# Symmetric scores computed once and transposed by DMA, attention accumulated transposed, feed-forward placed after each batch

## The chip, the core and the metric

The kernel runs on one core of a Trainium2 chip. The metric is the device time of one execution in microseconds (us). PE is the tensor engine (matmuls), PEld its weight loads, ACT the scalar engine, DVE the vector engine, POOL the general engine, SP the sync engine, which here does nothing but issue DMAs from its queue. The granted clock is the share of its full clock that PE was given in a stretch of time, 1.00 at most. A DMA is issued on its queue and lands some microseconds later. "L174" is line 174 of the kernel that the view belongs to, so the numbers differ from kernel to kernel.

## The reference

Per batch (8 batches, 3008 rows, width 256, `z` of width 64), an attention without softmax is gated by `u`; the 24064 rows that result go through a feed-forward layer of width 2048.

```python
scores = (1.0 / S) * np.matmul(z, z.transpose(0, 2, 1))
attn = np.maximum(scores, 0.0) ** 2
out = u * np.matmul(attn, v)
x = out.reshape(B * S, D)
h = x @ w_in
g = h * (1.0 / (1.0 + np.exp(-1.702 * h)))
return (g @ w_out).astype(np.float32)
```

The scores are `z` times its own transpose, so they are symmetric, and so is their squared positive part. Half of them would do.

## The kernel before

It runs in two stages: attention for all batches, with the gated result written to DRAM; then the feed-forward over blocks of 512 rows, each read back by two DMA transposes. A "unit" is 128x1024 scores: four key chunks of 128 for 256 queries. A unit is made by four matmuls with 64 contraction rows, in two pairs, each pair using the upper and the lower half of the array at once. ACT or DVE evicts it with a ReLU, and DVE or POOL squares it.

```python
        def scores(t):                       # 576 units
            # ... cut
            for p in range(2):
                for r_ in range(2):
                    j = 4 * q + 2 * p + r_
                    h0 = r_ * DQK
                    pe.matmul(sc[:, r_, p, :], ZT[h0:h0 + DQK, j * P:(j + 1) * P],
                        ZT[h0:h0 + DQK, isup * ISUP:(isup + 1) * ISUP], start=(p == 0), stop=(p == 1))
            if (t + 1) % DVE_RELU_EVERY == 0:
                dve.tensor_scalar(r, sc, 0.0, csc, ALU.max, ALU.mult)
            else:
                act.activation(r, sc, AF.Relu, scale=csc)
            (pool if (t + 1) % POOL_SQ_EVERY == 0 else dve).tensor_tensor(ap_, r, r, ALU.mult)   # abridged

        def attend(t):                       # the squared scores are the weights, V streams
            # ... cut
            for ib in range(NIBS):
                pe.matmul(O[:, ib, :], ap_[:, r_, p, ib * P:(ib + 1) * P], V16[:, j, :],
                    start=(j == 0 and ib == 0), stop=(j == NJ - 1 and ib == NIBS - 1))
            # ... after the last key chunk: X = O * u on DVE, and X goes to DRAM
```

Of the kernel before, what the change touches and what calls it, by code (L numbers as in the profile page):

```python
# [11 lines left out]
P = 128  # L12

DVE_RELU_EVERY = 5
POOL_SQ_EVERY = 4


@with_exitstack
def kernel(
# [8 lines left out]
):  # L28
    nc = tc.nc
# [10 lines left out]
    SPAD = NJ * P  # L40
    ISUP = 512
    NIS = SPAD // ISUP
    NIBS = ISUP // P
    NJP = NJ // 2
    NTOK = B * S
    TB = 512
    NTB = (NTOK + TB - 1) // TB
    NCC = D // P
    NFF = DFF // P
    NK = D // P  # L50
    NFG = 8
    FFG = NFF // NFG
    assert NTOK % P == 0

# [3 lines left out]
    dve = nc.vector  # L58
    act = nc.scalar
    pe = nc.tensor  # L60
    sp = nc.sync
    pool = nc.gpsimd

    const = ctx.enter_context(tc.tile_pool(name="const", bufs=1))
    ident = const.tile([P, P], F16, name="ident")
    make_identity(nc, ident)
    W1 = const.tile([P, NK, DFF], F16, name="W1")
    W2 = const.tile([P, NFF, D], F16, name="W2")

    dramp = ctx.enter_context(tc.tile_pool(name="dramp", bufs=1, space=bass.MemoryType.DRAM))  # L70
    xdram = dramp.tile([NTOK, D], F16, name="xdram")

    pxt = ctx.enter_context(tc.tile_pool(name="pxt", bufs=4))
    XTs = [None] * (NTB + 1)
    TBCs = [0] * (NTB + 1)

    def load_xt(tb, eng):
        if tb >= NTB or XTs[tb] is not None:
            return
        TBC = min(TB, NTOK - tb * TB)  # L80
        TBCs[tb] = TBC
        XT = pxt.tile([P, NCC, TB], F16, name="XT", tag="XT")
        XTs[tb] = XT
        for cc in range(NCC):
            eng.dma_start_transpose(  # L85
                XT[:, cc, :TBC],
                xdram[tb * TB:tb * TB + TBC, cc * P:(cc + 1) * P],
            )

    ISUP = 256  # L90
    NIS = SPAD // ISUP
    NIBS = ISUP // P
    UNITS = NJ // 4
    NU = NIS * UNITS
    GRP = 3
    LAG = 2 * GRP
    ZG = 8

    with (
        tc.tile_pool(name="pa", bufs=2) as pa,  # L100
        tc.tile_pool(name="pa1", bufs=1) as pa1,
        tc.tile_pool(name="pr", bufs=7) as pr,
        tc.tile_pool(name="ps_sc", bufs=3, space=bass.MemoryType.PSUM) as ps_sc,
        tc.tile_pool(name="ps_o", bufs=2, space=bass.MemoryType.PSUM) as ps_o,
        tc.manual_schedule(engines={mybir.EngineType.PE}),
    ):
        loads = {}
        zts = {}
        Xd = {}

        def load_batch(b):
            if b >= B:
                return
            zst = pa1.tile([P, NJ, DQK], F32, name="zst", tag="zst")
            vst = pa1.tile([P, NJ, D], F32, name="vst", tag="vst")
            if SREM:
                pool.memset(zst[SREM:, NJ - 1, :], 0.0)  # L117
                pool.memset(vst[SREM:, NJ - 1, :], 0.0)  # L118
            half = NJ // 2
            zd = z[b, :S0].rearrange("(n p) d -> p n d", p=P)  # L120
            sp.dma_start(zst[:, :half, :], zd[:, :half, :])
            sp.dma_start(zst[:, half:NJ - 1, :], zd[:, half:, :])
            if SREM:
                sp.dma_start(zst[:SREM, NJ - 1, :], z[b, S0:S].unsqueeze(1))
            sp.dma_start(vst[:, :NJ - 1, :], v[b, :S0].rearrange("(n p) c -> p n c", p=P))
            if SREM:
                sp.dma_start(vst[:SREM, NJ - 1, :], v[b, S0:S].unsqueeze(1))
            zst16 = pa.tile([P, NJ, 2, DQK], F16, name="zst16", tag="zst16")
            for h in range(2):
                js = slice(h * half, (h + 1) * half)  # L130
                for c in range(2):
                    dve.tensor_copy(zst16[:, js, c, :], zst[:, js, :])  # L132
            V16 = pa.tile([P, NJ, D], F16, name="V16", tag="V16", bufs=3)
            X = pa.tile([P, NJ, D], F16, name="X", tag="X")
            zts[b] = pa.tile([P, SPAD], F16, name="ZT", tag="ZT")
            casts = [(V16[:, 4 * q:4 * (q + 1), :], vst[:, 4 * q:4 * (q + 1), :]) for q in range(NJ // 4)]
            loads[b] = (zst16, V16, casts)
            Xd[b] = X

        def zt_part(b, g):  # L140
            zst16 = loads[b][0]
            ztp = ps_o.tile([P, ZG, P], F16, name="ztp", tag="O")
            for jj in range(ZG):
                pe.transpose(ztp[:, jj, :], zst16[:, g * ZG + jj, :, :], ident)  # L144
            act.activation(zts[b][:, g * ZG * P:(g + 1) * ZG * P], ztp, AF.Copy, scale=1.0)  # L145

        def v_cast(b):
            casts = loads[b][2]
            if casts:
                o, i_ = casts.pop(0)  # L150
                dve.tensor_copy(o, i_)  # L151

        def load_u(b, isup):
            ru = pa.tile([P, NIBS, D], F32, name="ru", tag="ru", bufs=4)
            lo = isup * ISUP
            hi = min(S, lo + ISUP)
            nfull = (hi - lo) // P
            sp.dma_start(
                ru[:, :nfull, :],
                u[b, lo:lo + nfull * P].rearrange("(n p) c -> p n c", p=P),  # L160
            )
            rem = (hi - lo) - nfull * P
            if rem > 0:
                sp.dma_start(ru[:rem, nfull, :], u[b, lo + nfull * P:hi].unsqueeze(1))
                pool.memset(ru[rem:, nfull, :], 0.0)
            return ru

        aps = {}
        Os = {}
        us = {}  # L170

        def scores(t):
            b, k = divmod(t, NU)
            isup, q = divmod(k, UNITS)  # L174
            ZT = zts[b]
            if q == 0:
                us[(b, isup)] = load_u(b, isup)
            sc = ps_sc.tile([P, 2, 2, ISUP], F32, name="sc", tag="sc")
            for p in range(2):
                for r_ in range(2):  # L180
                    j = 4 * q + 2 * p + r_
                    h0 = r_ * DQK
                    pe.matmul(  # L183
                        sc[:, r_, p, :],
                        ZT[h0:h0 + DQK, j * P:(j + 1) * P],
                        ZT[h0:h0 + DQK, isup * ISUP:(isup + 1) * ISUP],
                        start=(p == 0), stop=(p == 1),
                    )
            r = pr.tile([P, 2, 2, ISUP], F16, name="r", tag="r")
            if (t + 1) % DVE_RELU_EVERY == 0:  # L190
                dve.tensor_scalar(r, sc, 0.0, csc, ALU.max, ALU.mult)  # L191
            else:
                act.activation(r, sc, AF.Relu, scale=csc)  # L193
            ap_ = pr.tile([P, 2, 2, ISUP], F16, name="ap_", tag="ap_", bufs=11)
            aps[t] = ap_
            if (t + 1) % POOL_SQ_EVERY == 0:
                pool.tensor_tensor(ap_, r, r, ALU.mult)
            else:
                dve.tensor_tensor(ap_, r, r, ALU.mult)

        def attend(t):
            b, k = divmod(t, NU)
            isup, q = divmod(k, UNITS)
            ap_ = aps.pop(t)
            V16 = loads[b][1]
            if q == 0:
                Os[isup] = ps_o.tile([P, NIBS, D], F32, name="O", tag="O")
            O = Os[isup]
            for p in range(2):
                for r_ in range(2):  # L210
                    j = 4 * q + 2 * p + r_
                    for ib in range(NIBS):
                        pe.matmul(  # L213
                            O[:, ib, :],
                            ap_[:, r_, p, ib * P:(ib + 1) * P],
                            V16[:, j, :],
                            start=(j == 0 and ib == 0), stop=(j == NJ - 1 and ib == NIBS - 1),
                        )
            if q == UNITS - 1:
                X = Xd[b]  # L220
                ru = us.pop((b, isup))
                dve.tensor_tensor(X[:, isup * NIBS:(isup + 1) * NIBS, :], O, ru, ALU.mult)  # L222
                del Os[isup]
                if isup == NIS - 1:
                    sp.dma_start(
                        xdram[b * S:b * S + S0].rearrange("(n p) c -> p n c", p=P),
                        X[:, :NJ - 1, :],
                    )
                    if SREM:
                        sp.dma_start(xdram[b * S + S0:(b + 1) * S].unsqueeze(1), X[:SREM, NJ - 1, :])  # L230

        load_batch(0)
        for g in range(NJ // ZG):
            zt_part(0, g)
        load_batch(1)
# [114 lines left out]
```

## Time and profile before

| | before |
|---|---|
| time, median (range) | 1458.07 us (1457.97 to 1458.94), 3 runs |
| attention, as counted here (scores begin at 13.4 us, the first matmul with V comes at 21.9) | 26 to 766 us |
| feed-forward, as counted here (its first groups run from 765.8 us) | 776 to 1452 us |
| PE busy, whole span | 95% |

The first view is the page of the kernel before: the busy row of PE (us, share of the span, instructions), and the chain of work that ended last, by engine.

```profile
PE 1380.4 (95%) x11616; PEld 996.3 (68%) x11616; DVE 1177.3 (81%) x1195; ACT 847.4 (58%) x863; POOL 305.1 (21%) x176
...
PE 79%; DVE 11%; DMA 4%; issue 3%; ACT 2%; ACTq 1%; SPq 0%; DVEq 0%
```

Next the windows view of the kernel before, for its two stages: window, its length, busy us of each engine, granted clock, DMA share, GB/s.

```profile
26.00:766.00 740.00, 692.94 (x7029) 548.82 (x7030) 659.47 (x709) 454.99 (x474) 301.05 (x165) 0.97 0.31 88
776.00:1452.00 676.00, 673.62 (x4500) 439.22 (x4499) 507.18 (x470) 378.63 (x376) 0.00 (x0) 1.00 0.18 53
```

PE is the limit in both stages. In attention DVE is nearly as full: 659 of 740 us. A busy PE is not yet a PE at its best rate, so the rate has to be read from starts. The timeline of PE of the kernel before gives them (start, busy, what; in brackets the idle time before, and who ended it):

```profile
499.99 0.83 PE L183 MATMUL sc<-ZT 64*128 64x256 f16 x12
500.75 1.05 PE L213 MATMUL O<-V_3991,ap__6715 128*128 128x256 f16 x8
...
513.96 0.99 PE L183 MATMUL sc<-ZT 64*128 64x256 f16 x12 [3.44 <-DVE r L191]
```

Six score pairs take 500.75 - 499.99 = 0.76 us. The last line shows PE waiting 3.44 us for an eviction on DVE: that is what a full DVE costs.

### The profile page before, as it was taken

Reading aid. Unit: us, or ns where it says so; the run is one execution under the profiler, and the core shown is the slowest. Engines: PE = TensorE matmul, PEld = TensorE weight load, DVE = VectorE, ACT = ScalarE, POOL = GpSimd, SP = SyncE. Lnnn points to the kernel's source line nnn. Section 1 sums busy time; section 2 is a strip of 40 time slices with the busy share of each in tenths; the row PEclk is TensorE's granted clock in tenths of the full one; section 3 lists DMA queues with packets and bytes.
Section 4 is the critical chain, followed back from the end, with each engine's and each line's share of the span. In section 5 each row is a group of like instructions: output and inputs, shape, how many; then the busy total and the mean of one; then the engine's idle time right before and its main releaser. Section 6 shows DMA issues by size and latency. Waiting matters only on the chain.

```text
span 1456.5 us, 27175 instructions
## 1 busy us (share of the span) xinstructions
PE 1380.4 (95%) x11616; PEld 996.3 (68%) x11616; DVE 1177.3 (81%) x1195; ACT 847.4 (58%) x863; POOL 305.1 (21%) x176
## 2 busy tenths in 40 slices
PE   5888899999999999999997999999999999999998
PEld 3566677777777777777784666666666666666666
DVE  5989789898999988988985877777777777787775
ACT  4455565665666656666655556555555656565553
POOL 2333344343444433434340000000000000000000
PEclk9899899999999999999999999999999999999999
DMA  9734425124251111212102121211111111112111
GB/s 295 214 117 126 118 50 164 38 67 146 57 164 37 57 51 36 80 37 69 46 21 62 54 66 48 62 51 59 51 59 52 58 52 59 54 56 64 48 49 44
DMA packets 175691, 110.69 MB, mean 76 GB/s; under 512 B 78545, under 2 KB 174801, under 8 KB 175313
## 3 DMA queue, kind: packets, MB, share of 16 engines
q1 hardware_dynamic: 123632, 92.42, 21.2%
q10 hardware_dynamic: 51136, 12.33, 3.8%
q0 software_dynamic: 800, 4.19, 0.8%
q8 instruction: 91, 1.49, 0.4%
q14 instruction: 32, 0.25, 0.1%
HBM read 59.64 MB, written 36.96 MB: 66 GB/s over the span
## 4 chain that ended last, share of the span: by engine, by line
PE 79%; DVE 11%; DMA 4%; issue 3%; ACT 2%; ACTq 1%; SPq 0%; DVEq 0%
PE O L213 26%; PE hg L284 24%; PE yps L309 22%; PE sc L183 7%; DVE r L191 2%; DMA vst<-in_v_dram 2%; ACT r L193 1%; DVE X L222 1%; DMA xdram<-X 1%; ACTq L85 1%; DMA zst<-in_z_dram 1%; DVE V_1333 L151 0%; DVE zst_7973 L132 0%; DVE V_6649 L151 0%; DVE V_3991 L151 0%
## 5 line engine op out<-in xcount | busy, mean ns | idle before, releaser
L193 ACT ACTIVATE r<-sc 128x1024 f16<-128x1024 f32 x461 | 443.1, 1024 | 256.1 <-PE sc L183 237.0
L291 ACT ACTIVATE tsg<-hg 128x1024 f16<-128x1024 f32 x376 | 379.6, 1023 | 286.0 <-PE hg L284 180.9
L292 DVE TENSOR_TENSOR GT<-hg,tsg 128x1024 f16<-128x1024 f32 x376 | 447.0, 1221 | 113.6 <-ACT tsg L291 111.1
L284 PE MATMUL hg<-XT,W_63 128*128 128x512 f16 x1504 | 371.5, 379 | 9.6 <-DVE GT L292 9.5
L309 PE MATMUL yps<-W_64,GT 128*128 128x256 f16 x3008 | 374.1, 273 | 0.0
L309 PEld LDWEIGHTS <-GT 128*128 128x128 f16 x3008 | 294.2, 98 | 94.0
L284 PEld LDWEIGHTS <-W_63 128*128 128x128 f16 x1504 | 146.3, 97 | 151.3 <-issue 27.6
L183 PE MATMUL sc<-ZT 64*128 64x256 f16 x2304 | 165.0, 275 | 32.5 <-DVE r L191 24.2
L183 PEld LDWEIGHTS <-ZT 64*128 64x128 f16 x2304 | 98.5, 95 | 83.1 <-issue 71.5
L191 DVE TENSOR_SCALAR r<-sc 128x1024 f16<-128x1024 f32 x115 | 139.4, 1213 | 8.5 <-PE sc L183 8.5
L315 DVE TENSOR_SCALAR ysb<-yps 128x512 f32<-128x512 f32 x94 | 64.5, 686 | 64.5 <-PE yps L309 64.5
L222 DVE TENSOR_TENSOR X<-O,ru 128x512 f16<-128x512 f32 x96 | 65.3, 680 | 6.8 <-PE O L213 6.8
L145 ACT ACTIVATE ZT<-ztp 128x1024 f16<-128x1024 f16 x24 | 24.4, 1023 | 36.2 <-PE ztp L144 36.2
L144 PE MATMUL ztp<-ident,zst_97 128*128 128x128 f16 x24 | 2.9, 312 | 10.5 <-DVE zst_97 L132 10.5
L132 DVE CAST zst_97<-zst 128x768 f16<-128x768 f32 x4 | 2.1, 557 | 9.9 <-DMA zst<-in_z_dram 9.9
L144 PEld LDWEIGHTS <-zst_97 128*128 128x128 f16 x24 | 2.4, 144 | 10.8 <-DVE zst_97 L132 10.8
L291 ACT ACT_TABLE_LOAD x1 | 1.3, 1283 | 14.2 <-DMA xdram<-X 14.2
L118 POOL MEMSET vst<- 64x256 f32 x8 | 2.8, 344 | 27.5 <-DVE V_1333 L151 6.0
L117 POOL MEMSET zst<- 64x64 f32 x8 | 1.2, 146 | 30.5 <-DVE zst_97 L132 9.5
L151 DVE CAST V_1333<-vst 128x1024 f16<-128x1024 f32 x6 | 5.6, 966 | 0.9 <-DMA vst<-in_v_dram 0.9
L151 DVE CAST V_102<-vst 128x1024 f16<-128x1024 f32 x6 | 3.8, 689 | 2.9 <-DMA vst<-in_v_dram 2.9
L151 DVE CAST V_5320<-vst 128x1024 f16<-128x1024 f32 x6 | 5.6, 962 | 0.0
(1766 smaller groups left out, 1875.5 us busy)
## 6 DMA issues: line engine op xcount, KB each, us to landing
out_dram<-ysb SPq DMA_DIRECT2D x47, 512.0 KB, 2.9
vst<-in_v_dram SPq DMA_DIRECT2D x8, 2944.0 KB, 12.2
ru<-in_u_dram SPq DMA_DIRECT2D x88, 256.0 KB, 2.7
xdram<-X SPq DMA_DIRECT2D x8, 1472.0 KB, 7.0
zst<-in_z_dram SPq DMA_DIRECT2D x8, 384.0 KB, 4.0
zst<-in_z_dram SPq DMA_DIRECT2D x8, 352.0 KB, 4.8
w1s<-in_moe_w_in_dram POOLq DMA_DIRECT2D x1, 2048.0 KB, 10.6
w2s<-in_moe_w_out_dram POOLq DMA_DIRECT2D x1, 2048.0 KB, 12.0
```

The source lines that it names most:

```text
L145: act.activation(zts[b][:, g * ZG * P:(g + 1) * ZG * P], ztp, AF.Copy, scale=1.0)
L151: dve.tensor_copy(o, i_)
L183: pe.matmul(sc[:, r_, p, :], ZT[h0:h0 + DQK, j * P:(j + 1) * P], ZT[h0:h0 + DQK, isup * ISUP:(isup + 1) * ISUP], start=(p == 0), stop=(p = ...
L191: dve.tensor_scalar(r, sc, 0.0, csc, ALU.max, ALU.mult)
L193: act.activation(r, sc, AF.Relu, scale=csc)
L213: pe.matmul(O[:, ib, :], ap_[:, r_, p, ib * P:(ib + 1) * P], V16[:, j, :], start=(j == 0 and ib == 0), stop=(j == NJ - 1 and ib == NIBS - 1),)
L222: dve.tensor_tensor(X[:, isup * NIBS:(isup + 1) * NIBS, :], O, ru, ALU.mult)
L284: pe.matmul(hg[:, e, :TBC], W1[:, k, ff * P:(ff + 1) * P], XT[:, k, :TBC], start=(k == 0), stop=(k == NK - 1),)
L291: act.activation(tsg[:, :, :TBC], hg[:, :, :TBC], AF.Sigmoid, scale=1.702 / FSC)
L292: dve.tensor_tensor(GT[:, fg * FFG:(fg + 1) * FFG, :TBC], hg[:, :, :TBC], tsg[:, :, :TBC], ALU.mult,)
L309: pe.matmul(yps[:, s2, :], GT[:, ff, s * P:(s + 1) * P], W2[:, ff, :], start=(ff == 0), stop=(ff == NFF - 1),)
L315: dve.tensor_scalar(ysb[:, yy * 2:yy * 2 + ns2, :], yps[:, :ns2, :], 1.0 / FSC, None, ALU.mult)
```

## The change

The intent: compute a score unit only where the key chunk is not before the query chunk (336 units of 128 keys x 2 by 512 queries instead of 576), and get the mirrored ones by a DMA transpose from SBUF to SBUF. Let the squared scores stream (512 columns) and V be the weights, so that the output is accumulated transposed, which is the layout that the feed-forward wants; the trip through DRAM goes. Run the feed-forward after each batch, its first nine groups inside the last query chunk, and the next batch's first score units under its end. V's casts go to POOL, output evictions to ACT. The core of the diff, cuts marked:

```diff
+    def load_z(b):
+        # ... z by POOL's queue with a cast, written twice side by side
+        sp.dma_start_transpose(ZT[b], zst.rearrange("p n c d -> p (n c d)"))
+    def load_u(b, i):
+        # ... four DMAs of 64-column runs on SP, then 32x32 transposes on DVE
-            if (t + 1) % DVE_RELU_EVERY == 0:
+            if dve_relu and n == 2:
                 dve.tensor_scalar(rl, sc, 0.0, csc, ALU.max, ALU.mult)
             else:
                 act.activation(rl, sc, AF.Relu, scale=csc)
+            a = pa.tile([P, 2, CH], F16, name="a", tag="a", bufs=21)
+            (pool if sq[0] % 4 == 0 else dve).tensor_tensor(a, rl, rl, ALU.mult)
+            cj = jp // 2
+            if cj > i:
+                # ... t: the transposed tile of (i, cj)
+                if cj < NCH - 1:
+                    sp.dma_start_transpose(
+                        t[:, k0:k0 + 2].rearrange("p r g c -> p (r g) c"),
+                        a.rearrange("p r c -> p (r c)"),
+                    )
+                else:
+                    for r in range(2):
+                        sp.dma_start_transpose(t[:, :, k0 + r, :], a[:, r, :])
+    def weights(b, i, j):
+        cj, g = divmod(j, CB)
+        if cj >= i:
+            return unit[b, i, j // 2][:, j % 2, :width(i)]
+        t = TT[b, cj, i]
+        # ... the 512 columns of the mirrored unit
-                            O[:, ib, :],
-                            ap_[:, r_, p, ib * P:(ib + 1) * P],
-                            V16[:, j, :],
+                acc[c][:, :n], V16[b][:, j, c, :], weights(b, i, j),
+    SCHED = {
+        0: [(4, 3), (14, 3), (23, 2), (34, 2)],
+        # ... at which attention step of chunk i how many units of chunk i + 1 are computed
+    }
+    for b in range(B):
+        for i in range(NCH):
+            # ... attention of chunk i; in the last chunk, an up group at every fifth step
+        # ... load_z, load_v, load_u of the next batch
+        for q in range(HEAD, nup):
+            up_group(b, q)
+            if q >= LAGY:
+                down(b, *downs.pop(0))
+        while downs or nxt:
+            if nxt and n % 3 == 0:
+                scores(b + 1, nxt.pop(0), True)
+            if downs:
+                down(b, *downs.pop(0))
+            n += 1
-        xdram = dramp.tile([NTOK, D], F16, name="xdram")   # and its stores and transposes
```

A unit whose mirror lies in an ordinary query chunk is transposed whole (eight blocks of 128x128); one whose mirror lies in the last, short chunk in two halves (four blocks each). Per batch that is 20 whole and 20 half transposes, all issued by SP.

## The prediction

> **What bounds it now.** The tensor engine. The page's busy table has PE at 95% (DVE 81%, ACT 58%), and the chain that ended last is 79% PE. By stages (windows table, chain in order of time): 26 us of start, attention to 766 us, 10 us of hand-over (X to DRAM 6.5 us), feed-forward to 1452 us at 99% PE busy. In the timeline of PE, 24 attention matmuls of 256 columns take 2.73 us (114 ns each) and 6 score pairs 0.76 us (127 ns a pair). Attention therefore owes PE 4608 x 114 = 524 us plus 1152 x 127 = 146 us, 670 of its 740 us. The rest is a clock of 0.91 early on and waits for DVE, which in attention is 89% busy: evictions of 1.21 us, and squares of 0.68 us that grow to about 2.4 us beside Pool's.
>
> **What changes.**
> - Score units (128x1024) fall from 576 to 336. Score pairs now have 512 columns: 336 x about 235 ns (estimate from 127 ns at 256) = 79 us, saving 67.
> - Attention becomes 47 matmul slots of 512 columns per query chunk: 48 x 47 x 216 ns, less the short last chunks, = 477 us, saving 47. 216 ns is the trace's feed-forward rate at 512; the Trainium skill, "TensorE: Matmul & The Clock Gate", section "Back-to-back issue gap", has the same (N/2.4+2.5).
> - 240 evictions (1.02-1.21 us) and 240 squares go away; V casts go to Pool, output evictions to ACT.
> - The X round trip through DRAM and the hand-over go: 8 us. Feed-forward PE work is unchanged, about 680 us.
> - Added: 160 whole and 160 half-unit DMA transposes, all issued by SP. The trace's XT transposes, half a unit each, occupy their issuing queue 1.25 us; ordinary issues 0.38 us. If the excess scales with bytes, a whole unit takes 2.1 us: 20 x 2.1 + 20 x 1.25 = 67 us of SP per batch, about 90 with the other loads, in an attention phase of 75-80 us that starts with some of it done. Bandwidth suffices: XT moved 12.3 MB in 3.8% of 16 engines' span, 223 GB/s (the skill's "DMA: Bandwidth & Descriptors", section "Latency and other measured facts", has 261 GB/s); 63 MB need about 280 us of the span. Query chunks 3 and 4 should wait for the freshest, 0-10 us per batch.
> - Start: z through Pool's queue, one large transpose, twelve units of scores, V casts on Pool: about 38 us before attention streams, 12 worse.
>
> **Sum.** 477 + 79 + 680 = 1236; plus start 38, batch changes 8 x 3 = 24, transposes 8 x 3 = 24: about 1322 us.
>
> **Predicted: 1320 us, 8 in 10 between 1262 and 1390. Faster by over 2%: 0.89; within 2%: 0.05; slower: 0.06.**
>
> **What would show each step.** Right: PE at least 91% busy; attention matmuls 216 ns apart, 47 us less; PE score work about 80 us; DVE below 70% in attention; gaps of several us before attention matmuls, once or twice per batch, released by a DMA into the transposed tiles, with SP's queue nearly solid then; whole transposes near 2.1 us on the queue. Wrong: PE waiting for ACT or DVE inside attention, or a gap at each batch boundary.
>
> **What would make it wrong.** SBUF-to-SBUF transposes costing 3 us or more on SP: the queue would then be the limit, attention about 110 us per batch, and the gain mostly gone. Cheaper transposes with a smooth start give 1270. Pool's V casts holding DVE's squares, or a fuller PE being granted a lower clock, would cost tens of us.

## More of the kernel before

A program on one core gives one time per run; all runs told of here agree within about 1% with the others of their kernel and are counted as fast.

The feed-forward leaves the order of its matmuls to the scheduler:

```python
        for tb in range(NTB + 1):
            # ... load_xt(tb + 1): two DMA transposes of 512x128 from DRAM
            for fg in range(NFG):            # "up": 4 matmuls of 512 columns, a sigmoid, a product
                # ... cut
                act.activation(tsg, hg, AF.Sigmoid, scale=1.702 / FSC)
                dve.tensor_tensor(GT[:, fg * FFG:(fg + 1) * FFG, :TBC], hg, tsg, ALU.mult)
            # ... "down" of block tb - 1: 64 matmuls of 256 columns, evicted by DVE
```

Last, a piece of the chain of the kernel before in its feed-forward (start, length, what):

```profile
903.51 0.22 PE yps L309 x2
903.73 0.91 PE hg L284 x4
904.64 0.22 PE yps L309 x2
...
904.86 1.02 PE hg L284 x4
...
908.26 5.35 PE yps L309 x49
```

The scheduler's order runs up groups in bursts, with only two or three down matmuls between them, and then 49 down matmuls in a row. Within a burst a group of four comes every 1.1 to 1.4 us, about as fast as DVE can take its products (1.22 us each on the page).

## The result, and the profile after

| | before | after |
|---|---|---|
| time, median (range) | 1458.02 us (1457.44 to 1458.94), 4 runs | 1305.53 us (1304.05 to 1308.17), 4 runs |
| ratio of fast runs | | 0.8956 (95%: 0.8939 to 0.8972) |
| PE busy | 1380.4 us | 1249.3 us |

A ratio is the mean time of one kernel's fast runs over that of the other's of the same rounds, so it is not quite the ratio of the medians quoted. Of the 152 us between the medians, 131 are busy time of PE. The kernel before was timed again; its median lay between 1455.2 and 1457.9 us.

The page of the kernel after: the same two rows.

```profile
PE 1249.3 (96%) x7520; PEld 680.3 (52%) x7520; DVE 844.5 (65%) x820; ACT 728.8 (56%) x786; POOL 266.9 (20%) x237
...
PE 92%; DVE 2%; DMA 1%; POOL 1%; issue 1%; ACT 1%; ACTq 1%; SPq 0%; POOLq 0%
```

The windows of one batch of the kernel after, its attention and its feed-forward; columns as above.

```profile
517.20:595.00 77.80, 76.94 (x386) 32.10 (x385) 46.52 (x52) 39.09 (x41) 23.18 (x15) 1.00 0.88 151
595.00:675.20 80.20, 79.24 (x567) 53.42 (x565) 60.02 (x52) 52.47 (x59) 10.65 (x14) 1.00 0.33 92
```

A batch takes 158.0 us, and all of it is PE: 76.9 of 77.8 us and 79.2 of 80.2 us. DVE is at 46.5 of 77.8 us in attention, 60%, so it no longer paces PE. The lower clock that the prediction named as a danger did not come: 0.992 over the run, against 0.985 before. The chain of the kernel after gives the rates:

```profile
1176.84 0.75 PE sc L126 x6
...
1192.58 0.54 PE sc L126 x4
1193.12 0.21 PE o L186 x2
1193.34 10.03 PE o L174 x46
...
1226.07 0.86 PE hg L222 x4
1226.93 0.87 PE yp L245 x8
```

An attention matmul of 512 columns takes 10.03 / 46 = 218 ns. Three score pairs take 0.75 us, two take 0.54. The feed-forward is now an even 0.865 + 0.87 = 1.735 us per up group and half down tile, eight of which serve 512 rows: 13.88 us, against (1452 - 776) / 47 = 14.4 us before.

The sum of tensor work by these rates: attention 48 x 47 x 0.218, less 10 for the short last chunks, 482 us; scores 8 x (10 x 0.75 + 6 x 0.54) = 86 us (ten groups of three pairs and six of two in each batch); feed-forward 47 x 13.88 = 652 us. Together 1220 us. The first attention matmul is at 32.5 us, and the first batch is 10.8 us longer than a later one (168.8 against 158.0). At the seven batch ends PE waits 18 us in all for evictions and products (1.9 us at four of them, 3.3 to 3.6 at three). That makes 1281 us. The remaining 24 us or so are small losses that I did not break down.

Three views of the kernel after concern the transposes. The first is the whole list of PE's waits (total us, times, longest):

```profile
PE sc L126 <- DMA ZT<-zst: 19.6, 1, 19.6
PE sc L126 <- ACT rl L136: 19.5, 18, 4.3
PE o L174 <- POOL V_96 L97: 5.3, 3, 2.6
PE sc L126 <- DVE gt L231: 4.8, 7, 1.0
PE sc L126 <- DVE rl L134: 3.2, 9, 0.6
```

No wait of an attention matmul (`o`) for a transposed tile (`tt`) is among them. The second is the queue of SP in time, in the same batch (start, time from the first issue to the end of the last, DMAs):

```profile
511.70 13.11 SPq L148 DMA_TRANSPOSE tt<-a  x8
524.91 5.14 SPq L154 DMA_TRANSPOSE tt<-a  x4
530.16 8.66 SPq L148 DMA_TRANSPOSE tt<-a  x6
538.93 5.13 SPq L154 DMA_TRANSPOSE tt<-a  x4
...
569.26 5.14 SPq L154 DMA_TRANSPOSE tt<-a  x4
574.45 1.64 SPq L111 DMA_DIRECT2D uq<-in_u_dram  x3
576.40 3.78 SPq L81 DMA_TRANSPOSE ZT<-zst  x1
580.28 4.68 SPq L111 DMA_DIRECT2D uq<-in_u_dram  x7
```

A row joins issues of one line and includes the short waits between them. Taken one by one, issues fill 66.7 of the 73.3 us from 511.7 to 585, nearly the whole attention of the batch, and the longest pause is 1.1 us. The queue ends in time. The third gives the duration of one issue on that queue in ns (minimum/median/maximum), for the whole units, the halves and z:

```profile
L148 SPq DMA_TRANSPOSE tt<-a x160: 1231/1279/5829, 25.1 to 1191.3; - x160
...
L154 SPq DMA_TRANSPOSE tt<-a x160: 1188/1257/2715, 53.0 to 1204.2; - x160
...
L81 SPq DMA_TRANSPOSE ZT<-zst x8: 3684/3873/5561, 11.8 to 1048.9; - x8
```

Eight blocks cost 1.28 us and four blocks 1.26 us: halving a transpose of this size saves nothing. Twenty-four blocks cost 3.87 us, 0.16 us a block. The prediction had scaled with bytes from four blocks to eight and got 2.1 us.

### The profile page after: what moved, and what is told of

It is laid out like the page before. It is cut to its first block, busy times and chain, and to the rows that moved or that the text cites. A ratio compares the mean times of both kernels' runs of the same rounds, so it can differ in the third digit from the quotient of the medians.

```text
span 1306.3 us, 19043 instructions
## 1 busy us (share of the span) xinstructions
PE 1249.3 (96%) x7520; PEld 680.3 (52%) x7520; DVE 844.5 (65%) x820; ACT 728.8 (56%) x786; POOL 266.9 (20%) x237
## 3 DMA queue, kind: packets, MB, share of 16 engines
q1 hardware_dynamic: 405760, 119.07, 45.4%
## 4 chain that ended last, share of the span: by engine, by line
PE 92%; DVE 2%; DMA 1%; POOL 1%; issue 1%; ACT 1%; ACTq 1%; SPq 0%; POOLq 0%
PE o L174 36%; PE hg L222 25%; PE yp L245 25%; PE sc L126 6%; PE o L186 1%; DVE rl L134 1%; DVE gt L231 1%; POOL a L140 1%; DMA W_58<-in_moe_w_in_dram 1%; ACTq L260 1%; DMA zst<-in_z_dram 1%; ACT sg L230 0%; POOL V_96 L97 0%; DVE a L140 0%; DMA vst<-in_v_dram 0%
## 5 line engine op out<-in xcount | busy, mean ns | idle before, releaser
L231 DVE TENSOR_TENSOR gt<-hg,sg 128x1024 f16<-128x1024 f32 (+1 forms) x384 | 460.4, 1200 | 182.4 <-ACT sg L230 181.0
L230 ACT ACTIVATE sg<-hg 128x1024 f16<-128x1024 f32 (+1 forms) x384 | 386.0, 1005 | 274.6 <-PE hg L222 271.5
L136 ACT ACTIVATE rl<-sc 128x1024 f16<-128x1024 f32 x304 | 291.4, 1024 | 282.7 <-PE sc L126 256.0
L245 PE MATMUL yp<-W_59,gt 128*128 128x256 f16 x3008 | 383.0, 273 | 0.0
L222 PE MATMUL hg<-xt,W_58 128*128 128x512 f16 (+1 forms) x1408 | 354.5, 374 | 0.0
L245 PEld LDWEIGHTS <-gt 128*128 128x128 f16 x3008 | 292.5, 98 | 104.3 <-issue 7.5
L140 POOL TENSOR_TENSOR a<-rl 128x1024 f16<-128x1024 f16 x84 | 166.2, 1979 | 717.1 <-ACT rl L136 700.2
L140 DVE TENSOR_TENSOR a<-rl 128x1024 f16<-128x1024 f16 x252 | 230.9, 939 | 98.1 <-ACT rl L136 95.1
L222 PEld LDWEIGHTS <-W_58 128*128 128x128 f16 x1536 | 150.3, 98 | 108.7
L126 PE MATMUL sc<-ZT 64*128 64x512 f16 x672 | 104.7, 394 | 47.1 <-DMA ZT<-zst 19.6
L114 DVE STREAM_TRANSPOSE ut<-uq 128x1024 f32<-128x1024 f32 (+1 forms) x48 | 58.6, 1220 | 54.1 <-DMA uq<-in_u_dram 53.2
L174 PEld LDWEIGHTS <-V_96 128*128 128x128 f16 x276 | 26.3, 100 | 43.9 <-issue 10.1
L174 PEld LDWEIGHTS <-V_2475 128*128 128x128 f16 x276 | 26.3, 99 | 35.4 <-issue 7.6
L174 PEld LDWEIGHTS <-V_8743 128*128 128x128 f16 x276 | 26.1, 99 | 35.1 <-issue 7.1
L174 PEld LDWEIGHTS <-V_5609 128*128 128x128 f16 x276 | 25.9, 98 | 34.3 <-issue 5.3
L174 PEld LDWEIGHTS <-V_10321 128*128 128x128 f16 x276 | 25.9, 98 | 33.9 <-issue 5.3
L174 PEld LDWEIGHTS <-V_919 128*128 128x128 f16 x276 | 25.9, 98 | 33.9 <-issue 5.3
L174 PEld LDWEIGHTS <-V_7187 128*128 128x128 f16 x276 | 25.9, 98 | 33.9 <-issue 5.3
```

What stands on the lines that cost most here:

```text
L114: dve.transpose(ut[:, :, :n // QW, :].rearrange("p k q t -> p q k t"), uq[:, :n // QW])
L126: pe.matmul(sc[:, r, :], zt[h, 2 * jp + r, :], zt[h, i * CB:(i + 1) * CB, :], start=True, stop=True,)
L136: act.activation(rl, sc, AF.Relu, scale=csc)
L140: (pool if sq[0] % 4 == 0 else dve).tensor_tensor(a, rl, rl, ALU.mult)
L174: pe.matmul(acc[c][:, :n], V16[b][:, j, c, :], weights(b, i, j), start=(c == 0 and j == 0), stop=(c == 1 and j == NJ - 2),)
L222: pe.matmul(hg[:, e, :n], W1[:, c, ff * P:(ff + 1) * P], XT[b, i][:, c, :n], start=(c == 0), stop=(c == NCC - 1),)
```

## The experiments

Twelve kernels ran, all built on the kernel after except two. Theory A: the gain is tensor-engine work removed, together with waits. Rivals: B, it is the relief of ACT and DVE; C, it is the overlap of the stages. A further question was how close the SP queue is to being the limit.

### All scores computed, nothing transposed

```diff
-            if cj > i:
+            if False:
-        if cj >= i:
+        if True:
             return unit[b, i, j // 2][:, j % 2, :width(i)]
-        return [(i, jp) for jp in range(2 * i, NU)]
+        return [(i, jp) for jp in range(NU)]
+    SCHED = {i: [(4, 2), (12, 2), (19, 2), (26, 2), (33, 2), (40, 2)] for i in range(NCH - 1)}
-            if dve_relu and n == 2:
+            if (n == 2) if dve_relu else (jp % 4 == 3):
                 dve.tensor_scalar(rl, sc, 0.0, csc, ALU.max, ALU.mult)
     # and a: 26 buffers for 21, tt/gt: 11 for 14
```

> The changed kernel with all 576 score units computed and no unit transposed; the transposed accumulation and the order of the stages stay. Theory A (the gain is tensor-engine work): 240 more score pairs at 0.25 us each give +60 us, so 1350 to 1390 us, PE still over 93% busy. Theory B (the gain is mostly relief of ScalarE and VectorE, which then pace attention again): over 1420 us, with PE waiting for evictions inside attention. Attention per batch was 78 us; A says about 86, B over 92.

Measured: 1398.64 us (1397.95 to 1399.70), +93 us, between the two. A quarter of the units made during attention are evicted by DVE here, so that ACT does not carry all the added ones. The page's busy row of this kernel:

```profile
PE 1336.9 (96%) x8000; PEld 678.1 (49%) x8000; DVE 1172.4 (84%) x1120; ACT 854.7 (61%) x906; POOL 423.6 (30%) x297
```

PE's waits for evictions, from the waits view of the same kernel (total us, times, longest):

```profile
PE sc L126 <- ACT rl L136: 13.1, 20, 3.2
PE sc L126 <- DVE rl L134: 8.0, 24, 0.4
```

PE is busy 88 us longer (1336.9 against 1249.3) and still at 96%, and all its waits for ACT and DVE come to 28.3 us, against 27.5 in the kernel after. So these 93 us are tensor work: A holds for them, and B does not explain them. But the 84% of DVE is an average over stages. Inside attention DVE is full in this run: in the window from 560 to 618.5 us it is busy 58.36 of 58.50 us, PE 57.18. PE waits for it only about 0.36 us per query chunk there; with much less tensor work DVE would probably have paced the stage. The relief of DVE is thus not what the 93 us are made of, but without it they would probably not have come out whole. The 93 us exceed the 60 us expected of A because the pairs now come in groups of two, at 0.54 us a group: each batch has 30 groups of two where it had six of three and six of two inside attention, 16.2 - 7.7 = 8.5 us, 68 us in eight batches. The 18 groups more per batch also delay the matmuls behind them: seven attention matmuls after a group take 1.62 us from start to start, about 0.1 us more than seven in a long run, which makes some 15 us (an estimate from these two rates). About 10 us are not broken down. So the reuse of symmetry is worth 93 us, and the rest of the change about 59 us (1457.39 to 1398.64).

### Each whole transpose issued as two halves

```diff
-                    sp.dma_start_transpose(
-                        t[:, k0:k0 + 2].rearrange("p r g c -> p (r g) c"),
-                        a.rearrange("p r c -> p (r c)"),
-                    )
+                    for r in range(2):
+                        sp.dma_start_transpose(t[:, k0 + r], a[:, r, :])
```

> Each whole-unit transpose issued as two half-unit ones: same bytes, 60 issues of about 1.26 us per batch on the SP queue in place of 40, so a whole unit costs about 2.5 us of the queue, a little more than the prediction's 2.1 us. If the measured 1.28 us is why no wait for transposes was seen, but the prediction's model of the waits holds, the chunks 3 and 4 now wait up to 13 us per batch: +40 to +110 us. If the queue has slack that the model missed: within 1% of the changed kernel (1295 to 1320 us).

Measured: 1461.87 us (1460.14 to 1465.01), +156 us, above the 40 to 110 us expected. The whole gain is gone, with the same arithmetic and the same bytes. The queue of SP in the timeline of this kernel:

```profile
596.01 16.35 SPq L149 DMA_TRANSPOSE tt<-a  x12
612.47 5.13 SPq L152 DMA_TRANSPOSE tt<-a  x4
617.69 1.06 SPq L111 DMA_DIRECT2D uq<-in_u_dram  x2
618.86 10.36 SPq L149 DMA_TRANSPOSE tt<-a  x8
```

PE in the timeline of the same kernel:

```profile
625.32 1.87 PE L172 MATMUL o<-tt,V 128*128 128x512 f16 x4 [9.38 <-DMA tt<-a]
640.20 5.30 PE L172 MATMUL o<-tt,V 128*128 128x512 f16 x16 [3.27 <-DVE xt L194]
```

And its windows view around the first of these waits:

```profile
610.00:650.00 40.00, 27.35 (x114) 10.71 (x112) 7.05 (x9) 6.67 (x7) 3.49 (x3) 0.83 0.54 111
```

The queue is solid, and PE waits 9.4 us for a transposed tile, at the fourth query chunk, which is where the prediction had looked for it. The second wait is named a gate on DVE; the u that the gate needs comes over the same queue, behind the transposes (that link is read from the order of the queue, not tested). The DMA engines are at 54% in this window, and over the run the packets of SP's queue took no more of their time than before (39.6% of 1463 us, against 45.4% of 1306), so it is issue time and not bandwidth that is short. There is a second cost: in the gaps the granted clock falls (0.83 in this window; 0.953 over the run against 0.992), and the same 7520 matmuls are busy 1286.1 us in place of 1249.3, 37 us more. The Trainium skill, "TensorE: Matmul & The Clock Gate", Part 1, describes this: an idle PE drops to half its clock, and comes back only after some microseconds of work. The trace agrees: the granted clock is 0.50 from 620.0 to 630.2 us, that is from within the 9.4 us wait until about 5 us after it, and the first four matmuls after the wait take 1.87 us, where four take 1.03 elsewhere. The 156 us add up from PE's waits and this: 40 us for transposed tiles and 43 for gates (neither occurs in the kernel after), 22 more for ACT's evictions, 14 for products, and the 37 us of slower matmuls.

### Each whole transpose issued twice

```diff
+                    dup = pa.tile([P, 8, P], F16, name="dup", tag="dup", bufs=3)
+                    sp.dma_start_transpose(dup, a.rearrange("p r c -> p (r c)"))
                     sp.dma_start_transpose(
```

> Each whole-unit transpose issued a second time into a scratch tile: the same 60 issues per batch as with the split, and 42 MB more moved. If issue time on the queue is what could matter, it costs what the split costs, within 10 us. If bandwidth of the 16 DMA engines matters (they are 60% busy per batch now), it costs at least 30 us more than the split, and landing takes longer than the present 3.3 us.

Measured: 1533.38 us (1532.87 to 1536.67), +228 us, and 72 us more than the split. The expectation of "within 10 us" failed: with as many issues, more bytes cost more. In the batch looked at the DMA share was 0.85 to 0.91 for 80 us of attention, and the median issue of the second copy 1.33 us. The median landing of the halves did not change (2.5 us), that of the whole ones went from 3.3 to 3.4 us. Bytes count once the engines are this full, though I can't separate the queue's slower issues from the scratch tiles' reuse (three buffers).

### The same bytes through another queue

```diff
+                    dup = pa.tile([P, 8, P + 8], F16, name="dup", tag="dup", bufs=2)
+                    pool.dma_start(dup[:, :, :P], a.rearrange("p r (g c) -> p (r g) c", c=P))
```

> The changed kernel with every whole unit copied once more, as 1024 runs of 256 bytes, by an ordinary DMA issued by Pool: the bytes of the run with each whole transpose issued twice, with the SP queue's issues left as they were. If the queue's issue time alone makes attention wait: within 15 us of 1305. If the DMA engines' time counts as well (that run cost 72 us more than the split at the same number of issues, and with all feed-forward last the DMA share was 100% in attention): +30 to +100 us, with transposes taking longer than 1.28 us of the queue.

Measured: 1464.61 us (1461.09 to 1473.83), +159 us, but inconclusive. The median whole transpose on SP's queue grew from 1.28 to 1.93 us, so bytes do slow the queue. However, POOL issued the copies in its own order, between its squares, and PE waited 87 us for POOL's squares. The run does not say how much of the 159 us belongs to the bytes.

### No overlap of the stages at the ends of a batch

```diff
-    HEAD = 9
+    HEAD = 0
-            if nxt and n % 3 == 0:
+            if nxt and not downs:
```

> The changed kernel without the overlap of stages: no feed-forward group inside the last query chunk, and the first twelve score units of the next batch only after the last down-projection. Theory A: only the twelve units' evictions become exposed, about 8 us at each of 7 batch ends: +40 to +75 us. Theory C (overlap of attention with feed-forward is the main source of the gain): over +100 us, with gaps spread over the feed-forward stage too. If the overlap is worth nothing: within 15 us of 1305.

Measured: 1366.62 us (1365.82 to 1369.14), +61 us, within A's range. From the waits view of this kernel:

```profile
PE sc L126 <- ACT rl L136: 42.5, 56, 4.3
```

The kernel after has 19.5 us and 18 times on this line; the waits that came are at the batch ends. The granted clock is 0.971, and PE is busy 29.5 us longer with the same matmuls (1278.8 us). Overlap at the ends is worth 61 us, but it is not the main source.

### All feed-forward after all attention

```diff
+    XD = dramp.tile([B * NCH, P, NCC, CH], F16, name="XD")
     # ZT and V16: two buffers; tt/gt 13 for 14; xt 5 for 8; the next batch's z and V loaded in its chunk 2
-        5: [],
+        5: [(4, 3), (14, 3), (23, 3), (34, 3)],      # the next batch's first units
+            act.dma_start(XD[b * NCH + i][:, :, :n], XT[b, i][:, :, :n])
     # ... all feed-forward in one loop at the end, its blocks read back from XD
```

> The changed kernel with its parts kept, but all attention first and all feed-forward after it, as in the kernel before: the gated output goes through DRAM already transposed, and the next batch's first twelve score units lie inside the last query chunk. If the place of the feed-forward is worth nothing in itself: 1285 to 1315 us, as batch ends lose their 4 us gaps. If the feed-forward's real service is the time it leaves to the SP queue (about 71 us of issues per batch, against 70 us of tensor work per batch in attention alone): attention waits for transposes as in the split, 1330 to 1400 us, with the queue nearly solid and PE gaps released by a transpose or by the late u loads behind them.

Measured: 1434.90 us (1432.75 to 1436.83), +129 us, above the 1330 to 1400 us expected: nearly all of the gain goes. Attention alone now takes about 91 us per batch ((760 - 35) / 8). The windows view of this kernel within attention:

```profile
300.00:600.00 300.00, 241.07 (x1158) 93.33 (x1158) 130.02 (x160) 123.54 (x130) 99.74 (x90) 0.91 1.03 185
```

PE's two longest waits in that attention, from the waits view:

```profile
PE o L176 <- DVE xt L198: 58.3, 18, 7.6
PE o L176 <- DMA tt<-a: 49.1, 7, 8.7
```

The DMA share is 103% (the packets' times, summed and divided by the time of 16 engines: by this measure nothing is left), PE is busy 80% of the time at a clock of 0.91. In the kernel after the share averages 60% over a batch, 88% in attention and 33% in the feed-forward. So the feed-forward of each batch is the time in which loads and transposes catch up. That placing it there is worth over 100 us is shown for this form of the kernel, which also has fewer buffers and a trip of the output through DRAM. The expectation had the SP queue as the reason, and this run has both the queue (issues fill 260 of these 300 us) and the DMA engines full.

### The same, with u's bytes taken away

```diff
-            sp.dma_start(uq[k * QW:(k + 1) * QW, :n // QW]. ... , src[:, :, cs])
+            if b == 0 and i == 0:
+                sp.dma_start(uq[k * QW:(k + 1) * QW, :n // QW]. ... , src[:, :, cs])
+            else:
+                few = pu.tile([P, 1, NCC * QW], F32, name="few", tag="few", bufs=8)
+                sp.dma_start(few[k * QW:(k + 1) * QW], src[:, :1, cs])
```

> The run with all feed-forward last, with u's bytes taken away but not its issues: after the first chunk each load of u brings 64 columns of 32 rows into a scratch tile and the first chunk's u is used again (a wrong result on purpose). The DMA share there was 100% through attention, with PE waiting 49 us for transposes and 58 us for gates, which themselves wait for u. If the count of issues on the SP queue is what makes attention longer when it stands alone: within 20 us of 1435, PE still waiting for transposes. If it is the DMA engines' time, or u arriving late behind other issues: 1310 to 1370, DMA share in attention clearly under 100% and most of the waits gone.

Measured: 1449.87 us (1448.38 to 1450.68). Its output is wrong, which doesn't matter for the time. PE's waits for transposes and gates are gone and the DMA share falls to 0.82 to 0.88, as the second expectation said; but the time does not fall. PE now waits 103 us for evictions on ACT instead, which in turn are held up by other things, transposes and V's loads among them. Neither expectation was met whole: the time is within the first one's 20 us, but without its waits for transposes. Which resource ends the wait in the kernel with all attention first stays open; taking one of them away only brought up the next.

### The kernel before, with the after's order of feed-forward matmuls

Two runs, one with the output eviction left on DVE, one with it on ACT.

```diff
+        tc.manual_schedule(engines={mybir.EngineType.PE}),
-        for tb in range(NTB + 1):
-            # ... scheduler's order
+        for q in range(NTB * NFG):
+            tb, fg = divmod(q, NFG)
+            up(tb, fg)                        # four matmuls of 512
+            if q >= NFG + 1:
+                down(*downs.pop(0))           # half a tile: eight of 256
     # and GT, the up groups' output: three buffers for two
     # second run: act.activation(ysb, yps, AF.Copy, ...) for dve.tensor_scalar(ysb, yps, ...)
```

> The kernel before, with nothing changed but the order of its feed-forward on the tensor engine: strictly one up group (four matmuls of 512) and then half a down tile (eight of 256), as in the changed kernel, in place of the scheduler's order. The feed-forward took 14.47 us per 512 tokens before and takes 13.9 after, which the prediction had as unchanged. If the order is the cause: 1440 to 1447 us. If the move of the output eviction from VectorE to ScalarE is: within 4 us of 1458.

> As the run with only the order of the feed-forward changed, and the output eviction on ScalarE in place of VectorE. If the order alone was the cause, within 4 us of that run; if the eviction was, 1440 to 1447 us here and about 1458 there.

Measured: 1436.59 us (1434.00 to 1437.11) and 1435.39 us (1433.69 to 1438.25), against 1456.02 for the kernel before: -19 and -21 us, a little below the 1440 to 1447 us expected of the order. The order does it; where the output is evicted does not matter. With this order three of GT's blocks are in use at a time, so the runs give it a third buffer, and the two were not separated. The chain of the first of these kernels, to hold against the bursts shown of the kernel before:

```profile
900.72 0.86 PE hg L284 x4
901.59 0.87 PE yps L305 x8
902.46 0.86 PE hg L284 x4
903.32 0.87 PE yps L305 x8
```

### The start and the batch ends

Three runs tried for a version that beats both. First, V's casts of the first batch on DVE and more staging for V:

```diff
-            vst = pu.tile([P, VB, D], F32, name="vst", tag="vst")
+            vst = pu.tile([P, VB, D], F32, name="vst", tag="vst", bufs=4)
-                pool.tensor_copy(
+                (pool if b else dve).tensor_copy(
```

> The changed kernel with the first batch's V casts on VectorE in place of Pool, and four buffers in place of two for V's staging, so that V's loads don't wait for the casts. The first batch's stretch is 10.8 us longer than a later one, with PE waiting for Pool's casts and for evictions that wait for Pool's squares. If those casts are the cause: 1293 to 1299 us. If the weights' load on the same queue is: within 4 us of 1305.

Measured: 1304.05 us (1303.57 to 1306.31), no difference. The waits for casts are gone, but the large first transpose now occupies the queue for 10.5 us in place of 5.6, so the first scores come at 26.4 us and not at 19.6. Second, the next batch's first scores earlier:

```diff
+            if nxt and q in (36, 42):
+                scores(b + 1, nxt.pop(0), True)
             up_group(b, q)
-            if nxt and n % 3 == 0:
+            if nxt and n % 4 == 0:
```

> The changed kernel with two of the four groups of the next batch's first score units put 6 and 12 feed-forward steps before the last up group, and the other two spread over the last down tiles. The chain shows about 4 us at each batch end in which PE waits for VectorE's evictions and squares of these units. If those waits go: 7 x 3 to 4 us, so 1277 to 1287 us, and the SP queue starts a batch's transposes some 10 us earlier. If they only move into the feed-forward (VectorE is 85% busy there): within 8 us of 1305.

Measured: 1306.51 us (1306.27 to 1306.94), no difference: the waits of about 1 us now stand in the feed-forward, where a score group must wait for the accumulators that the up groups hold. Third, both, with the weights' load held back:

```diff
+    for w in (W1, W2):       # each load must wait for this small write
+        for k in range(P // QW):
+            pool.tensor_copy(w[k * QW:(k + 1) * QW, 0, 0:1], unit[0, 0, 11][k * QW:(k + 1) * QW, 0, 0:1])
```

> As the run with the earlier score groups, and with the start changed: first batch's V casts on VectorE, four buffers for V's staging, and the weights' load held back until the last of the first twelve score units is squared. In the run with only the casts moved the large first transpose took 10.5 us of the queue in place of 5.6 us, beside the weights' 4 MB. If that traffic was the cause: the first scores start before 20 us and the first batch loses its waits for casts, 8 to 14 us under the run with only the earlier groups, about 1270 us.

Measured: 1313.40 us (1312.40 to 1314.67), 7 us worse than the run before it. The first scores do start at 16.2 us, and the large transpose takes 3.8 us, so the weights' traffic was what stretched it. But PE then waits 5.6 and 2.0 us for evictions on DVE, which stand behind V's casts in its queue, and the first attention matmul comes at 33.9 us, no earlier than the 32.5 of the kernel after. And one wait of 15.5 us follows, which ends at 66.7 us and which neither of the two other runs has. The chain leads from it through ACT and DVE to a load of u that was issued at 48.8 us and landed after 14.8 us, where the median is 3.0: the weights that were held back land from 46.8 to 63.3 us, beside it. The traffic was moved onto the next load that PE needed. No version beat the kernel after.

## Why the prediction was right, point by point

The time was right: 1320 predicted, 1305.5 measured, within the range. The main mechanism was right: PE bound before and after, and fewer, longer streams of columns on it.

- *Attention matmuls 216 ns apart.* Right: 218 ns. The term was 477 us and is 482. (The section of the Trainium skill that the prediction names, "Back-to-back issue gap" of "TensorE: Matmul & The Clock Gate", gives its formula for a matmul by itself, and about 131 ns per matmul for a stream at this width. The streams of this trace do not come near 131; the formula held.)
- *Score pairs 235 ns, 79 us.* Nearly: 250 to 270 ns, 86 us. Three pairs of 512 take what six of 256 took (0.75 and 0.76 us). Three pairs at the full rate of 216 ns would take 0.65; each switch between paired and full matmuls costs about 0.1 us, whatever the width, and a group of two spreads it over fewer pairs.
- *Feed-forward unchanged, 680 us.* Wrong. The new order alone saves 19 to 21 us in the kernel before; by the chain's rates the term is 652 us.
- *A whole transpose 2.1 us of the queue; 24 us of waits.* Wrong in the step that scaled with bytes. It measured 1.28 us, the same as a half, and PE waits for no transpose. "SP's queue nearly solid" was right.
- *The queue's danger.* The prediction named 3 us as the cost at which the gain is "mostly gone". The split, at two issues of 1.26 us, lost 156 us, all of it. So the price of 24 us put on 2.1 us was probably far too low; the term came out small only because the issue was cheaper than thought, which is luck. The model left out what follows from a gap: a lower clock and late u.
- *"Bandwidth suffices", 280 us of the engines' time for 63 MB.* The conclusion held, by less than thought: SP's queue took 45.4% of 1306 us here and 16.7% of 1396 us without the transposes, which leaves about 360 us for them (an estimate, the difference of two kernels). In attention the DMA share is 88%, and the runs with more bytes show that little was left.
- *Start, 38 us.* Somewhat low: 32.5 us to the first attention matmul, and a first batch 10.8 us longer than a later one, with 9.2 us of PE's waits and a clock of 0.96.
- *Batch ends, 24 us.* Somewhat high: 18 us of waits. *DVE under 70% in attention:* right, 60%. *PE at least 91%:* right, 96%.
- *What the feed-forward's place is for.* The prediction counted 8 us for the hand-over and nothing else. The run with all feed-forward last shows that its place is worth over 100 us in that form; attention alone keeps SP's queue and the DMA engines full there, and which of them counts stays open.

That the sum came within 17 us is partly luck: the feed-forward and the transposes were put 52 us too high, the batch ends 6 us, while attention, scores and start were 17 us too low together, and 24 us of losses were in no term.

In nested steps: before to all scores computed, -59 us, of which the feed-forward's order accounts for about 20 by its own run; all scores to the kernel after, -93 us. The split of the other 39 us (longer streams, no hand-over, fewer waits, a longer start) was not run. PE's waits for DVE and ACT are 58 us in the kernel before (its start left out) and 28 us with all scores computed, so for this part B is not excluded.

## What to carry to other kernels

When work moves to DMA, cost the issuing queue as an engine of its own: count its issues, take one issue's duration from a trace at the very size used, and set the sum against the shortest stage that waits for it, not against the whole run. A queue that is full but on time shows no wait at all; splitting its issues shows how near the edge it is. And a stage that needs little data next to one that needs much is worth interleaving, even where both are bound by the same engine.

## What the Trainium skill lacked or had wrong

- The issue time of an SBUF-to-SBUF transpose at working size: "DMA: Bandwidth & Descriptors", section "DMA Transpose (X-bar)", gives none; "VectorE: DVE Perf Modes", section "The three transpose paths", has one time for a single block of 128x128 and does not say what part of it is issue. Here: 1.26 us for four blocks of 128x128, 1.28 us for eight, 3.87 us for twenty-four.
- "Advanced Engine Details and Errata", section "X-Bar Transpose (TRN2)", says "TRN2 transpose DMAs are as fast as regular DMAs". From issue to landing that holds here (2.5 us for a half unit of 128 KB, 3.1 us for a load of u of 128 KB from DRAM). On the issuing queue it does not: 1.26 us for the half unit, against 0.49 us for the load of u.
- "Trainium Kernel Development and Optimization", section "Key Constraints", says that issuing DMAs from several engines only saves the sequencer's issue time. That is what was scarce here, so "only" misleads: 160 issues more on one queue, at the same bytes, cost 156 us.
- "TensorE: Matmul & The Clock Gate", Part 3, puts a packed set of matmuls at one matmul plus about 4 ns per further tile. No page puts a time on switching to such pairs from full matmuls and back: three pairs of 512 columns took 0.75 us and two 0.54 us, about 0.1 us a group more than pairs at 216 ns would, and the matmuls after a group start about 0.1 us later again.
